# Per-chunk attention products as 64x64x64 tiles on quarters of the array

## The chip, the cores and the metric

The program runs on one core of a Trainium2 chip. The metric is the time of one execution on the device in microseconds, as the median of several runs. The profile is of one further execution of the same program; its span runs from its first to its last instruction. TensorE multiplies matrices out of SBUF into PSUM (8 banks of 2 KB in each of 128 partitions), VectorE, ScalarE and GpSimd work element by element, and SyncE's queue (SP) issues most of the transfers.

## What is computed

Attention within chunks of 64 positions, then two feed-forward stages:

```
scores = q_c k_c^T / 8                     # per batch, head, chunk: 64 x 64, head_dim 64
attn   = softmax(scores);  out = attn v_c  # 8 batches, 8 heads, 576 positions = 9 chunks
h      = x @ w_in                          # 4608 tokens, 512 -> 1024
ln     = layernorm(h * softmax(h)) * g_ln
y      = ln @ w_out                        # 1024 -> 512
result = (silu(y @ w_gate) * (y @ w_val)) @ w_out2   # 512 -> 1536 -> 512
```

## The kernel before

The 4608 tokens are 36 tiles of 128 tokens. A tile holds two chunks of 64 positions, and for each chunk all 8 heads. The first phase (to about 600 us) takes the tiles through attention, the first feed-forward stage and, in groups of three tiles, the product with w_out; it also converts weights and writes split copies of them to memory. The second phase is the gated stage and the output product.

The order of the first phase is written out by hand (`tc.manual_schedule()`, line 485), one call of `first_slot(t)` for the first four tiles and of `slot(t)` for the rest (lines 569 to 646). Each engine works its own list in the order in which the calls stand there; what one engine needs of another is waited for through semaphores that the framework sets, and matmuls into a PSUM bank also wait for readers of the same tile's data in that bank. A slot of the steady part has on TensorE, in this order: the scores of tile t+2 (line 258), the hidden product of tile t (line 327, 24 matmuls of 512 columns), the transposes of the layernorm of tile t-1 (line 397), probabilities times values of tile t+1 (line 300), 32 matmuls of the product with w_out (line 145), and the transposes of the probabilities of tile t+2 (line 290). In `first_slot` values stand directly behind scores, ahead of the softmax.

Both products on chunks run in fp32. With head_dim 64 and chunks of 64 a product of one head and one chunk is 64 x 64 x 64. The kernel handles the two chunks of a head in one call: the stationary operand has 128 rows (the two chunks' 64 rows each, one chunk below the other) and 64 columns, and the moving operand is block diagonal, 128 rows by 2 x 64 columns, with zeros where row and column belong to different chunks. These operands are `kbd` for the keys and `pbd` for the transposed probabilities (lines 237 and 238, two buffers each), zeroed once at the start (lines 411 to 413) and then filled in their diagonal blocks: `kbd` by two transfers per tile (line 245), `pbd` by two ScalarE copies of 64 partitions each (line 293). Even heads write the lower 64 PSUM partitions, odd heads the upper (`tile_position`). An fp32 matmul call of this form has two weight-load and two matmul records in the trace. Scores (`s`) and outputs (`o`) take the two one-bank buffers of the pool `ps_a` in turn.

`softmax` takes the row maximum and subtracts it on VectorE (lines 267 and 269) and exponentiates on ScalarE (272); `softmax_b` sums, and scales on GpSimd (282); `p_transpose` transposes on TensorE. `x_split` reads `o` twice, a copy on ScalarE (309) and a subtraction on VectorE (311), and makes the two-part input of the hidden product. `ln_max`, `ln_exp`, `ln_b` and `ln_c` (lines 339 to 381) follow the hidden product on VectorE, ScalarE and GpSimd. The PSUM pool `ps_y` has two buffers, which the products with w_out (emptied on ScalarE, line 151) and the transposed probabilities take in turn.

Of the kernel before, what the change touches and what calls it, by code (L numbers as in the profile page):

```python
# [8 lines left out]
F32 = mybir.dt.float32  # L9
# [4 lines left out]
AF = mybir.ActivationFunctionType  # L14
ALU = mybir.AluOpType
AX = mybir.AxisListType

P = 128
CH = 64
# [6 lines left out]
def attn_moe_moe2_kernel(  # L26
# [13 lines left out]
    nc = tc.nc  # L40
    NT = qT.shape[0]
    NG = NT // GT
    H = 8
    NP = H // 2
# [175 lines left out]
    with ExitStack() as ph1:  # L220
        wpool = ph1.enter_context(tc.tile_pool(name="wpool", bufs=1))
        wA = wblock(wpool, "A", 2 * KD)
        att = ph1.enter_context(tc.tile_pool(name="att", bufs=2))
        fix = ph1.enter_context(tc.tile_pool(name="fix", bufs=1))
        sm = ph1.enter_context(tc.tile_pool(name="sm", bufs=4))
        xp = ph1.enter_context(tc.tile_pool(name="xp", bufs=2))
        hp_ = ph1.enter_context(tc.tile_pool(name="hp", bufs=2))
        stage = ph1.enter_context(tc.tile_pool(name="stage", bufs=2))
        ps_a = ph1.enter_context(tc.tile_pool(name="ps_a", bufs=2, space=bass.MemoryType.PSUM))
        ps_h = ph1.enter_context(tc.tile_pool(name="ps_h", bufs=1, space=bass.MemoryType.PSUM))  # L230
        ps_t = ph1.enter_context(tc.tile_pool(name="ps_t", bufs=1, space=bass.MemoryType.PSUM))
        ps_y = ph1.enter_context(tc.tile_pool(name="ps_y", bufs=2, space=bass.MemoryType.PSUM))
# [1 line left out]
        qt, kt, vt, st, xt = {}, {}, {}, {}, {}  # L234


        kbd = [fix.tile([P, H, 2, CH], F32, name=f"kbd{i}") for i in range(2)]
        pbd = [fix.tile([P, H, 2, CH], F32, name=f"pbd{i}") for i in range(2)]

        def load_qk(t):  # L240
            qt[t] = att.tile([P, H, CH], F32, tag="qt", name="qt")
            nc.sync.dma_start(out=qt[t], in_=qT[t].rearrange("p (h i) -> p h i", h=H))
            for c in range(2):
                r = slice(c * CH, (c + 1) * CH)
                nc.sync.dma_start(
                    out=kbd[t % 2][r, :, c, :], in_=kT[t, r].rearrange("p (h j) -> p h j", h=H)
                )

        def load_v(t):
            vt[t] = att.tile([P, H, CH], F32, tag="vt", name="vt")  # L250
            nc.sync.dma_start(out=vt[t], in_=v[t].rearrange("p (h d) -> p h d", h=H))

        def scores(t):
            s = ps_a.tile([P, NP, 2, CH], F32, tag="a", name="s")
            q = qt.pop(t)
            for h in range(H):
                n, b = divmod(h, 2)
                nc.tensor.matmul(  # L258
                    s[b * CH:(b + 1) * CH, n], lhsT=q[:, h, :], rhs=kbd[t % 2][:, h],
                    start=True, stop=True, tile_position=(0, b * CH),  # L260
                )
            st[t] = s

        def softmax(t):
            s = st[t].rearrange("p n c j -> p (n c) j")
            mx = sm.tile([P, H], F32, tag="mx", name="mx")
            nc.vector.tensor_reduce(out=mx, in_=s, axis=AX.X, op=ALU.max)
            e = att.tile([P, H, CH], F32, tag="e", name="e")
            nc.vector.tensor_tensor(
                out=e, in0=s, in1=mx.unsqueeze(2).to_broadcast([P, H, CH]), op=ALU.subtract  # L270
            )
            nc.scalar.activation(out=e, in_=e, func=AF.Exp, scale=SCALE)
            st[t] = e
# [12 lines left out]
        def p_transpose(t):  # L286
            e = st.pop(t).rearrange("p (n c) j -> p n (c j)", c=2)
            pt = ps_y.tile([P, H, CH], F32, tag="y", name="pt")
            for n in range(NP):
                nc.tensor.transpose(pt[:, 2 * n:2 * n + 2].rearrange("p h i -> p (h i)"), e[:, n], ident)  # L290
            for c in range(2):
                r = slice(c * CH, (c + 1) * CH)
                nc.scalar.activation(out=pbd[t % 2][r, :, c], in_=pt[r], func=AF.Copy)

        def pv(t):
            vv = vt.pop(t)
            o = ps_a.tile([P, NP, 2, CH], F32, tag="a", name="o")
            for h in range(H):
                n, b = divmod(h, 2)
                nc.tensor.matmul(  # L300
                    o[b * CH:(b + 1) * CH, n], lhsT=vv[:, h, :], rhs=pbd[t % 2][:, h],
                    start=True, stop=True, tile_position=(0, b * CH),
                )
            st["o", t] = o

        def x_split(t):
            o = st.pop(("o", t)).rearrange("p n c i -> p n (c i)")
            x = xp.tile([P, 2, KD, P], F32R, tag="x", name="x")
            nc.scalar.activation(out=x[:, 0], in_=o, func=AF.Copy)
            xt[t] = x  # L310
            low = lambda: nc.vector.tensor_tensor(
                out=x[:, 1], in0=o, in1=x[:, 0].bitcast(F32), op=ALU.subtract
            )
            return low

# [92 lines left out]

        make_identity(nc, ident)
        nc.gpsimd.memset(mhalf, -0.5)  # L410
        for i in range(2):
            nc.gpsimd.memset(kbd[i], 0.0)
            nc.vector.memset(pbd[i], 0.0)
        rblk = [
            pool.tile([P, KD, DM], I64, tag=f"C{i}", name=f"rin{i}")
            for i, pool in enumerate((wpool, lastp))
# [5 lines left out]
        load_in(0)  # L422
        load_in(1)
        load_qk(0)
        load_in(2)
        load_qk(1)
        load_in(3)
        load_v(0)
# [12 lines left out]
        def y_upto(t):  # L441

            return max(0, min((NG - 1) * KD * NY, (t - GT) * KD * NY // GT)) if t >= W_OUT else 0
# [48 lines left out]
        word(1)  # L492
        add(1)
        scores(0)
        mag(2)
        clp(POOL, 2)
        high(0)
        rnd(2)
        high(1)
        softmax(0)  # L500
        rest(DVE, 0)
        word(2)
# [6 lines left out]
        high(2)  # L509
        rnd(4)  # L510
        p_transpose(0)
        word(3)
        add(3)
        rest(DVE, 2)
        scores(1)
        mag(5)
        clp(POOL, 5)
        word(4)
        add(4)
        high(3)  # L520
        pv(0)
        x_low = x_split(0)
        rest(DVE, 3)
        x_low()
# [17 lines left out]
        add(7)  # L542
        high(6)
        softmax(1)
        high(7)
        rest(DVE, 6)
        softmax_b(1)
        rest(DVE, 7)
        hidden(0, (1,))
        p_transpose(1)  # L550

        wB = wblock(lastp, "B", KF)
        raws = {0: w_raw(0)}
        load_qk(2)
        load_v(2)
        load_qk(3)
# [12 lines left out]
        def slot(t, todo2):  # L569
# [5 lines left out]
            if ahead:  # L575
                scores(t + 2)
                if t + 4 < NT:
                    load_qk(t + 4)
                softmax(t + 2)
# [12 lines left out]
            if t + 1 < NT:  # L592
                pv(t + 1)
                if t + 3 < NT:
                    load_v(t + 3)
                x_low = x_split(t + 1)
# [16 lines left out]
            if t + 2 < NT:  # L613
                raws[t + 2] = w_raw(t + 2)
                p_transpose(t + 2)
            return w_rest(todo, cs)

        def first_slot(t, todo2):

            todo = w_todo(t)  # L620
            cs = conv.pop(t)
            scores(t + 2)
            load_qk(t + 4)
            for k, steps in todo2:
                steps[1]()
            pv(t + 1)
            load_v(t + 3)
            softmax(t + 2)
            cs[:1] = [conv_c(c) for c in conv_b(cs[:1])]
            x_low = x_split(t + 1)  # L630
            softmax_b(t + 2)
            x_low()
            conv_start(t + 1)
            if t > 0:
                hidden(t)
            ln_max(t)
            ln_exp(t)
            cs[1:] = [conv_c(c) for c in conv_b(cs[1:])]
            ln_low = ln_T(t - 1) if t >= 1 else None
            ln_b(t)  # L640
            p_transpose(t + 2)
            if ln_low:
                ln_low()
            ln_c(t)
            raws[t + 2] = w_raw(t + 2)
            return w_rest(todo, cs)
# [17 lines left out]
        n = y_upto(NT - 1)  # L664
# [236 lines left out]
```

## Time and profile before

| | |
|---|---|
| three runs | 1431.06, 1431.95, 1433.1 us |
| median | 1431.95 us |
| the profiled execution's own time | 1430.28 us |
| its span | 1428.5 us |
| mean granted TensorE clock | 0.989 of full |
| TensorE busy, matmuls | 1376.6 us (96%) |
| TensorE busy, weight loads | 1251.2 us (88%) |
| VectorE, ScalarE, GpSimd busy | 846.2, 585.9, 469.8 us |
| scores and values matmuls (lines 258, 300) | 44.2 and 42.2 us busy |

Busy time is the union of an engine's records. A matmul's record goes on after the next one has begun, so a stage of TensorE is read from its first start to the first start of the next stage. A granted clock of 1.00 is 2.4 GHz and of 0.50 is 1.2 GHz; values between are a mean over a stretch with both. In a group's or a timeline's row, a bracket or the columns behind the bar name the idle time ahead of it and what ended it ("issue" is nothing that the profile shows).

### The profile page before, as it was taken

How to read it: one execution, taken by the hardware profiler on the slowest of the kernel's cores; microseconds unless marked ns; L12 is line 12 of the kernel's file. 1: busy time of each engine (PE TensorE's matmuls, PEld its weight loads, DVE VectorE, ACT ScalarE, POOL GpSimd, SP SyncE). 2: the span in 40 equal slices, each digit the busy share in tenths (PEclk: the TensorE clock that was granted, in tenths of full speed). 3: DMA queues.
4: the chain of work that ended last, by engine and by line, in shares of the span. 5: the costliest groups of instructions: out<-in, count | busy, mean ns of one | idle time of the engine just before them, and what ended most of it. 6: DMA issues, size and time to landing. Idle time of an engine off the chain costs nothing.

```text
span 1428.5 us, 21447 instructions
## 1 busy us (share of the span) xinstructions
PE 1376.6 (96%) x7920; PEld 1251.2 (88%) x7920; DVE 846.2 (59%) x1534; ACT 585.9 (41%) x1172; POOL 469.8 (33%) x591
## 2 busy tenths in 40 slices
PE   4789999999999999899999999999999999999998
PEld 3668888888888889899989998999999899989997
DVE  7876677777676666554474456445544644474442
ACT  5754555655555555432332333323323323233231
POOL 5643444444453443421231223213212412141120
PEclk9799999999999999999999999999999999999999
DMA  7433655546475553876645473455455454735531
GB/s 257 126 94 99 186 163 167 179 128 202 132 208 158 151 163 113 329 299 240 224 146 196 167 246 137 171 202 203 147 203 205 153 192 165 247 125 179 203 106 45
DMA packets 123128, 252.02 MB, mean 176 GB/s; under 512 B 45712, under 2 KB 79504, under 8 KB 113808
## 3 DMA queue, kind: packets, MB, share of 16 engines
q1 hardware_dynamic: 116112, 241.21, 50.6%
q10 hardware_dynamic: 6912, 9.44, 1.9%
q8 instruction: 63, 1.03, 0.3%
q14 instruction: 41, 0.34, 0.1%
HBM read 203.43 MB, written 47.19 MB: 175 GB/s over the span
## 4 chain that ended last, share of the span: by engine, by line
PE 76%; DVE 2%; ACT 1%; POOL 1%; issue 1%; ACTq 0%; DVEq 0%; POOLq 0%
PE o L799 14%; PE pa L733 11%; PE pd L733 10%; PE pc L733 10%; PE h L327 8%; PE y L145 7%; PE tail L799 7%; PE pb L733 5%; PE s L258 1%; PE o L300 1%; PE tr L397 1%; PE pt L290 1%; DVE so L357 0%; DVE nm L339 0%; ACT eh L346 0%
## 5 line engine op out<-in xcount | busy, mean ns | idle before, releaser
L327 PE MATMUL h<-wA,x 128*128 128x512 f32 x864 | 214.3, 404 | 6.3 <-DVE wA L480 2.5
L145 PE MATMUL y<-lnT,wB 128*128 128x384 f32 x1152 | 211.8, 340 | 5.2 <-DVE lnT L405 3.8
L145 PEld LDWEIGHTS y<-lnT,wB 128*128 128x128 f32 x1152 | 200.5, 190 | 11.6 <-issue 5.3
L790 POOL TENSOR_TENSOR uflow<-sa,uflow 128x384 fp32r<-128x384 f32 x72 | 73.4, 1019 | 414.4 <-ACT uflow L761 393.2
L327 PEld LDWEIGHTS h<-wA,x 128*128 128x128 f32 x864 | 163.3, 193 | 48.2 <-issue 5.8
L733 PE MATMUL pa<-yk,wsa 128*128 128x384 f32 x864 | 175.0, 337 | 0.8 <-DVE osb L816 0.8
L733 PE MATMUL pd<-yk,wsb 128*128 128x384 f32 x864 | 172.9, 334 | 0.0
L790 DVE TENSOR_TENSOR uflow<-sb,uflow 128x128 fp32r<-128x128 f32 x72 | 28.1, 391 | 228.9 <-ACT uflow L788 228.9
L733 PEld LDWEIGHTS pa<-yk,wsa 128*128 128x128 f32 x864 | 153.2, 188 | 7.6 <-DVE osb L816 2.9
L733 PEld LDWEIGHTS pd<-yk,wsb 128*128 128x128 f32 x864 | 151.8, 188 | 0.0
L769 POOL TENSOR_TENSOR u<-u,p 128x384 f32<-128x384 f32 x72 | 72.9, 1013 | 193.5 <-DVE u L768 189.6
L758 ACT ACTIVATE p<-pa 128x384 f32<-128x384 f32 x72 | 35.4, 492 | 232.7 <-PE pa L733 231.0
L799 PE MATMUL o<-wo,uflow 128*128 128x512 f32 x504 | 122.8, 392 | 0.0
L799 PEld LDWEIGHTS o<-wo,uflow 128*128 128x128 f32 x504 | 94.0, 188 | 18.1
L346 ACT ACTIVATE eh<-h,nm 128x1024 f32<-128x1024 f32 x36 | 40.1, 1115 | 155.0 <-DVE nm L339 155.0
L771 ACT ACTIVATE sa<-pa 128x384 f32<-128x384 f32 x72 | 35.5, 492 | 150.0 <-PE pa L733 150.0
L799 PE MATMUL o<-uflow 128*128 128x512 f32 x360 | 87.4, 391 | 0.0
L733 PE MATMUL pc<-yk,wsa 128*128 128x384 f32 x432 | 86.4, 334 | 0.0
L733 PE MATMUL pb<-yk,wsa 128*128 128x384 f32 x432 | 86.4, 334 | 0.0
L733 PE MATMUL pc<-yk,wsb 128*128 128x384 f32 x432 | 86.4, 334 | 0.0
L772 DVE TENSOR_TENSOR sa<-pa,sa 128x384 f32<-128x384 f32 x72 | 40.1, 557 | 71.6 <-ACT sa L771 71.6
L799 PEld LDWEIGHTS o<-uflow 128*128 128x128 f32 x360 | 67.2, 188 | 13.2
(107 smaller groups left out, 2361.6 us busy)
## 6 DMA issues: line engine op xcount, KB each, us to landing
wsa<-ws SPq DMA_DIRECT2D x72, 1024.0 KB, 5.0
wsb<-ws SPq DMA_DIRECT2D x72, 768.0 KB, 5.9
ws<-shi SPq DMA_DIRECT2D x12, 896.0 KB, 4.5
raw<-in_moe_w_out SPq DMA_DIRECT2D x20, 512.0 KB, 5.1
qt<-in_q SPq DMA_DIRECT2D x36, 256.0 KB, 4.7
kbd<-in_k SPq DMA_DIRECT2D x72, 128.0 KB, 4.9
vt<-in_v SPq DMA_DIRECT2D x36, 256.0 KB, 2.8
y<-ysb ACTq DMA_DIRECT2D x48, 192.0 KB, 2.1
```

What stands on the lines that cost most here:

```text
L145: nc.tensor.matmul(ys[u], lhsT=wB[:, f, a, d * P:(d + 1) * P], rhs=lnT[m][:, b, f, :], start=(n == 0), stop=(n == NY - 1),)
L258: nc.tensor.matmul(s[b * CH:(b + 1) * CH, n], lhsT=q[:, h, :], rhs=kbd[t % 2][:, h], start=True, stop=True, tile_position=(0, b * CH),)
L290: nc.tensor.transpose(pt[:, 2 * n:2 * n + 2].rearrange("p h i -> p (h i)"), e[:, n], ident)
L327: nc.tensor.matmul(h[:, n * DM:(n + 1) * DM], lhsT=x[:, a, k, :], rhs=wA[:, n * KD + k, b, :], start=(i == 0), stop=(i == 3 * KD - 1),)
L346: nc.scalar.activation(out=e, in_=h, func=AF.Exp, bias=nm, accum_out=se)
L733: nc.tensor.matmul(ps, lhsT=w[:, a, kk * P:(kk + 1) * P], rhs=yk[:, i, b, kk], start=(first and n == 0), stop=(n == 5), skip_group_check=True,
L758: nc.scalar.activation(out=p1, in_=psA, func=AF.Copy)
L769: nc.gpsimd.tensor_tensor(out=u3, in0=u3, in1=p5, op=ALU.add)
L771: nc.scalar.activation(out=sa, in_=psA, func=AF.Sigmoid)
L772: nc.vector.tensor_tensor(out=sa, in0=psA, in1=sa, op=ALU.mult)
L790: sub = lambda eng, o, x, h: eng.tensor_tensor(out=o, in0=x, in1=h.bitcast(F32), op=ALU.subtract)
L799: nc.tensor.matmul(o, lhsT=u[:, a, i * P:(i + 1) * P], rhs=wout(f)[:, b], start=(j0 and j == 0), stop=(j1 and j == 2),)
```

## The change

Each of the two products becomes 16 calls of 64 x 64 x 64 per tile, one for each head and chunk. A call uses 64 rows of the array (the chunk's) and 64 columns (by the head's parity). Keys and transposed probabilities are kept without zeros in [128, 8, 64] tiles, loaded by one transfer and written by one copy; the block-diagonal tiles, their memsets and their pool go. In PSUM a chunk has a bank of its own; scores take one half of each of the two banks and outputs the other half, in one tile that lives through the phase. The softmax and `x_split` read the new order of chunks and heads through other views.

```diff
-        ps_a = ph1.enter_context(tc.tile_pool(name="ps_a", bufs=2, space=bass.MemoryType.PSUM))
+        ps_a = ph1.enter_context(tc.tile_pool(name="ps_a", bufs=1, space=bass.MemoryType.PSUM))
...
-        kbd = [fix.tile([P, H, 2, CH], F32, name=f"kbd{i}") for i in range(2)]
-        pbd = [fix.tile([P, H, 2, CH], F32, name=f"pbd{i}") for i in range(2)]
+        so_ps = ps_a.tile([P, 2, 2, NP, CH], F32, name="so_ps")
+        s_ps, o_ps = so_ps[:, :, 0], so_ps[:, :, 1]
+        quads = [(n, c, b) for n in range(NP) for c in range(2) for b in range(2)]
+
+        def quad(out, lhsT, rhs, n, c, b):
+
+            r, h = slice(c * CH, (c + 1) * CH), 2 * n + b
+            nc.tensor.matmul(
+                out[b * CH:(b + 1) * CH, c, n], lhsT=lhsT[r, h], rhs=rhs[r, h],
+                start=True, stop=True, tile_position=(c * CH, b * CH),
+            )
...
-            for c in range(2):
-                r = slice(c * CH, (c + 1) * CH)
-                nc.sync.dma_start(
-                    out=kbd[t % 2][r, :, c, :], in_=kT[t, r].rearrange("p (h j) -> p h j", h=H)
-                )
+            kt[t] = att.tile([P, H, CH], F32, tag="kt", name="kt")
+            nc.sync.dma_start(out=kt[t], in_=kT[t].rearrange("p (h j) -> p h j", h=H))
...
-            s = ps_a.tile([P, NP, 2, CH], F32, tag="a", name="s")
-            q = qt.pop(t)
-            for h in range(H):
-                n, b = divmod(h, 2)
-                nc.tensor.matmul(
-                    s[b * CH:(b + 1) * CH, n], lhsT=q[:, h, :], rhs=kbd[t % 2][:, h],
-                    start=True, stop=True, tile_position=(0, b * CH),
-                )
-            st[t] = s
+            q, k = qt.pop(t), kt.pop(t)
+            for i in quads:
+                quad(s_ps, q, k, *i)
...
-            s = st[t].rearrange("p n c j -> p (n c) j")
-            mx = sm.tile([P, H], F32, tag="mx", name="mx")
-            nc.vector.tensor_reduce(out=mx, in_=s, axis=AX.X, op=ALU.max)
+            mx = sm.tile([P, 2, NP], F32, tag="mx", name="mx")
+            nc.vector.tensor_reduce(out=mx, in_=s_ps, axis=AX.X, op=ALU.max)
             e = att.tile([P, H, CH], F32, tag="e", name="e")
             nc.vector.tensor_tensor(
-                out=e, in0=s, in1=mx.unsqueeze(2).to_broadcast([P, H, CH]), op=ALU.subtract
+                out=e.rearrange("p (n c) j -> p c n j", c=2), in0=s_ps,
+                in1=mx.unsqueeze(3).to_broadcast([P, 2, NP, CH]), op=ALU.subtract,
             )
...
-            for c in range(2):
-                r = slice(c * CH, (c + 1) * CH)
-                nc.scalar.activation(out=pbd[t % 2][r, :, c], in_=pt[r], func=AF.Copy)
+            p = att.tile([P, H, CH], F32, tag="p", name="p")
+            nc.scalar.activation(out=p, in_=pt, func=AF.Copy)
+            st["p", t] = p
...
-            vv = vt.pop(t)
-            o = ps_a.tile([P, NP, 2, CH], F32, tag="a", name="o")
-            for h in range(H):
-                n, b = divmod(h, 2)
-                nc.tensor.matmul(
-                    o[b * CH:(b + 1) * CH, n], lhsT=vv[:, h, :], rhs=pbd[t % 2][:, h],
-                    start=True, stop=True, tile_position=(0, b * CH),
-                )
-            st["o", t] = o
+            vv, p = vt.pop(t), st.pop(("p", t))
+            for i in quads:
+                quad(o_ps, vv, p, *i)
...
-            o = st.pop(("o", t)).rearrange("p n c i -> p n (c i)")
+            o = o_ps.rearrange("p c n i -> p n c i")
             x = xp.tile([P, 2, KD, P], F32R, tag="x", name="x")
-            nc.scalar.activation(out=x[:, 0], in_=o, func=AF.Copy)
+            hi, lo = (x[:, i].rearrange("p n (c i) -> p n c i", c=2) for i in range(2))
+            nc.scalar.activation(out=hi, in_=o, func=AF.Copy)
...
-        for i in range(2):
-            nc.gpsimd.memset(kbd[i], 0.0)
-            nc.vector.memset(pbd[i], 0.0)
```

## Rows read from the trace of the kernel before

**Rows 1.** Stretches (us): length, busy time (records) per engine, PE clock, DMA.

```profile
30.00:60.00 30.00, 20.36 (x130) 15.83 (x130) 23.25 (x41) 19.42 (x35) 17.08 (x21) 0.78 0.36 106
102.09:545.26 443.17, 432.00 (x2897) 378.77 (x2897) 306.25 (x547) 240.88 (x424) 190.38 (x296) 1.00 0.53 158
600.00:1428.00 828.00, 823.91 (x4323) 768.55 (x4321) 426.64 (x809) 256.84 (x594) 194.71 (x184) 1.00 0.52 185
```

**Rows 2.** Timeline, TensorE, one steady slot: start us, us, what, records.

```profile
301.18 1.09 PE L258 MATMUL s<-kbd,qt 128*64 128x128 f32 x16
302.21 5.75 PE L327 MATMUL h<-wA,x 128*128 128x512 f32 x24
...
308.76 1.09 PE L300 MATMUL o<-pbd,vt 128*64 128x128 f32 x16
309.79 5.82 PE L145 MATMUL y<-lnT,wB 128*128 128x384 f32 x32
```

**Rows 3.** Groups, TensorE, 100 to 560 us: records | busy us, mean ns.

```profile
L300 PE MATMUL o<-pbd,vt 128*64 128x128 f32 x480 | 32.8, 279 | 0.0
L258 PE MATMUL s<-kbd,qt 128*64 128x128 f32 x464 | 32.2, 282 | 0.0
```

**Rows 4.** Short stretches, records on tile s: length, PE busy, loads, VectorE.

```profile
301.17:301.20 0.03, 0.02 (x2) 0.02 (x2) 0.00 (x0) 1.00 0.00 0
...
301.33:301.36 0.03, 0.03 (x4) 0.03 (x4) 0.00 (x0) 1.00 0.00 0
...
301.44:301.47 0.03, 0.03 (x6) 0.03 (x4) 0.00 (x0) 1.00 0.00 0
```

**Rows 5.** Groups, weight loads (PEld), 100 to 560 us.

```profile
L327 PEld LDWEIGHTS h<-wA,x 128*128 128x128 f32 x727 | 134.9, 189 | 32.8 <-issue 5.1
...
L258 PEld LDWEIGHTS s<-kbd,qt 128*64 128x64 f32 x464 | 25.1, 138 | 4.8 <-issue 4.8
```

**Rows 6.** Waits, TensorE, 100 to 560 us: total us, times, longest.

```profile
PE pt L290 <- ACT ysb L151: 6.0, 3, 2.6
PE pt L290 <- POOL rs L380: 3.5, 4, 1.5
PE pt L290 <- POOL so L381: 1.5, 1, 1.5
```

**Rows 7.** Chain that ended last, 361 to 376 us: start, us.

```profile
361.81 5.70 PE h L327 x24
...
367.53 1.24 DVE nm L339
...
375.45 0.38 ACT ysb L151
```

**Rows 8.** A stretch after a long wait, and the chain behind it.

```profile
469.80:471.40 1.60, 1.60 (x18) 1.24 (x17) 0.00 (x0) 1.18 (x2) 0.88 (x2) 0.65 1.03 337
...
471.42 6.76 PE h L327 x24
```

**Rows 9.** Timeline of the same slot: readers of scores and outputs, next scores.

```profile
303.05 0.69 DVE L269 TENSOR_TENSOR e<-s,mx 128x512 f32<-128x512 f32 x1
...
313.57 0.68 DVE L311 TENSOR_TENSOR x<-o,x 128x512 fp32r<-128x512 f32 x1
...
315.98 1.09 PE L258 MATMUL s<-kbd,qt 128*64 128x128 f32 x16
```

**Rows 10.** Timeline of the start: idle time before and its releaser in brackets.

```profile
0.89 1.84 POOL L412 MEMSET kbd<- 128x1024 f32 x2
...
7.83 1.97 PE L258 MATMUL s<-kbd,qt 128*64 128x128 f32 x16 [7.83 <-DMA kbd<-in_k]
...
9.85 0.69 DVE L267 TENSOR_REDUCE mx<-s 128x8 f32<-128x512 f32 x1 [0.88 <-PE s L258]
```

**Rows 11.** Timeline of the opening, 72 to 75 us, ScalarE and TensorE.

```profile
72.16 1.19 ACT L293 ACTIVATE pbd<-pt 64x512 f32<-64x512 f32 x2
...
73.40 1.13 PE L300 MATMUL o<-pbd,vt 128*64 128x128 f32 x16 [2.26 <-ACT pbd L293]
```

More of the change, by code (lines that the diff above doesn't have):

```diff
@@ L223, in attn_moe_moe2_kernel @@
         att = ph1.enter_context(tc.tile_pool(name="att", bufs=2))
-        fix = ph1.enter_context(tc.tile_pool(name="fix", bufs=1))
         sm = ph1.enter_context(tc.tile_pool(name="sm", bufs=4))
@@ L290, in p_transpose @@
                 nc.tensor.transpose(pt[:, 2 * n:2 * n + 2].rearrange("p h i -> p (h i)"), e[:, n], ident)
-            for c in range(2):
-                r = slice(c * CH, (c + 1) * CH)
-                nc.scalar.activation(out=pbd[t % 2][r, :, c], in_=pt[r], func=AF.Copy)
+            p = att.tile([P, H, CH], F32, tag="p", name="p")
+            nc.scalar.activation(out=p, in_=pt, func=AF.Copy)
+            st["p", t] = p
         def pv(t):
-            vv = vt.pop(t)
-            o = ps_a.tile([P, NP, 2, CH], F32, tag="a", name="o")
-            for h in range(H):
-                n, b = divmod(h, 2)
-                nc.tensor.matmul(
-                    o[b * CH:(b + 1) * CH, n], lhsT=vv[:, h, :], rhs=pbd[t % 2][:, h],
-                    start=True, stop=True, tile_position=(0, b * CH),
-                )
-            st["o", t] = o
+            vv, p = vt.pop(t), st.pop(("p", t))
+            for i in quads:
+                quad(o_ps, vv, p, *i)
         def x_split(t):
-            o = st.pop(("o", t)).rearrange("p n c i -> p n (c i)")
+            o = o_ps.rearrange("p c n i -> p n c i")
             x = xp.tile([P, 2, KD, P], F32R, tag="x", name="x")
-            nc.scalar.activation(out=x[:, 0], in_=o, func=AF.Copy)
+            hi, lo = (x[:, i].rearrange("p n (c i) -> p n c i", c=2) for i in range(2))
+            nc.scalar.activation(out=hi, in_=o, func=AF.Copy)
             xt[t] = x
             low = lambda: nc.vector.tensor_tensor(
-                out=x[:, 1], in0=o, in1=x[:, 0].bitcast(F32), op=ALU.subtract
+                out=lo, in0=o, in1=hi.bitcast(F32), op=ALU.subtract
             )
```

## The prediction

> **What bounds the kernel now.** I read the table of stretches first [rows 1]. From 102 to 545 us, the 30 steady slots of the first phase, TensorE is busy 432.0 of 443.2 us at full clock, while VectorE has 306, ScalarE 241 and GpSimd 190: TensorE's own work sets the pace. From 600 us on it is busy 824 of 828 us, and nothing there is edited. Only in the opening is another engine tighter: between 30 and 60 us VectorE is busy 23.3 of 30 us, TensorE 20.4, at a granted clock of 0.78.
>
> Next I read one slot on TensorE in order of time [rows 2]. The scores begin at 301.18 and the hidden matmuls at 302.21: the score stage holds TensorE for 1.03 us. The values stage runs from 308.76 to 309.79: 1.03 us again. The stretch has 29 score stages and 30 values stages (464 and 480 records of 16) [rows 3], about 60 us in all. That is what the change can shorten.
>
> Then I looked inside one score stage with very short stretches [rows 4]; the counts are records that touch the stretch. Two begin at 301.18, two more by 301.36, two more by 301.47. So records begin in twos, one two per 0.11 us: 8 steps, 0.88 us. The other 0.15 us of the stage lies at its two ends, where the first weights are loaded and the last results leave. Each of the 8 calls has two records of 128 columns. I read a two as the left and the right half of the array at work together, each passing 128 columns in a step.
>
> **The change, part by part.**
>
> *The two products.* A stage goes from 8 calls with 128 rows, 64 weight columns and 128 moving columns to 16 calls of 64 by 64 by 64, four places in place of two. Records go from 16 to 32. If four run together, there are again 8 steps, each with 64 columns, so half as long: 0.055 us. The weight load must fit under it. A 128-column load has a mean of 189 ns and a 64-column load 138 ns [rows 5], so 64 columns are worth 51 ns: just under the step. I take 0.06 us, since there is almost nothing to spare: 8 x 0.06 = 0.48 in place of 0.88, a gain of 0.40 us per stage. The ends: 0.44 us with 0.055, and 0 with the step of today.
> All of a score stage's gain reaches the end, as the hidden matmuls follow at once: 29 x 0.40 = 11.6 us. A values stage's gain is lost where the probability transposes later wait for something else than TensorE. They do so eight times in the stretch [rows 6]. The chain of waits shows why [rows 7]: it leaves TensorE at the end of the hidden matmuls (367.5), passes through the maximum on VectorE and a line of work on ScalarE, and comes back when ScalarE has emptied a PSUM tile at 375.8. The values stage lies beside that chain. So 30 - 8 = 22 stages count: 22 x 0.40 = 8.8 us.
> Those eight waits grow by 0.40 us each. After one of them, at 469.8, the clock was granted at 0.65 and a score stage took 1.6 us, the hidden matmuls behind it 6.76 us in place of 5.7 [rows 8]: 1.6 us lost in all. I set 1 us against the gain for more of this; ends 0 and 3.
>
> *Scores and outputs share two PSUM banks.* A matmul into a bank waits for the readers of the bank's other half. Scores would now wait for the subtraction that ends x_split two slots before: it ends at 314.25 and the scores begin at 315.98, 1.7 us of room, of which the shorter values stage takes 0.4. The values product waits for the softmax's subtraction, which ends at 303.74, while the product begins at 308.76 [rows 2, 9]. Behind those waits stands all of TensorE, but the room covers them: 0. In the first four slots values come directly behind scores, so that the row maximum now waits for both; the two shorter stages together last about as long as one did: 0.
>
> *Zeros and copies.* The memsets of kbd hold GpSimd from 0.89 to 2.73 us, ahead of the key loads. The first scores begin at 7.83, when the keys land, and VectorE then waits 0.88 us for them [rows 10]. An earlier key load and a shorter stage at half clock can take that wait away and no more than a little beyond: I take 1 us; ends 0 and 3. VectorE's memsets of pbd lie before its first job. The two half copies into pbd (1.19 us together) become one copy over 128 partitions with as many columns as one of them, 0.6 us less on ScalarE. Where values wait for them, as at 73.4 (2.26 us) [rows 11], the opening's tighter VectorE is next: I take 0.5 us in all; ends 0 and 2.
> The key load is one transfer in place of two, so that the SP queue has one issue less per slot; it lands well ahead of its use after the start, and its cover is the slots it is loaded ahead: 0. VectorE and ScalarE read and write as many elements as before in another order; their room in the stretch [rows 1] hides what that might cost.
>
> *Sum.* 11.6 + 8.8 + 1 + 0.5 - 1 = 20.9 us. The profiled execution took 1430.28 us (span 1428.5), which gives 1409.4. It lies 1.67 us under the median of the three runs, 1431.95. Against the median: **1411 us**.
>
> **The rivals.**
>
> *A, four places are no faster than two.* A two could be the two records of one call, one call at a time; then 16 calls make 16 steps of 0.055 us, 0.88 us as now. Left are the start and the copies: 1430.5. For it: 8 calls in 8 steps fit as well. Against it: one record needs the step for its own 128 columns, and two of them in one place would share it.
> The Trainium skill, page "TensorE: Matmul & The Clock Gate", Part 3, says that matmuls start and end strictly in program order and only weight loads are pulled ahead. By that, a call's second half would hold back the next call, and the new stage would have 17 steps, 0.935 us: 59 x 0.055 = 3.2 us more than in A, about 1434. The trace speaks against it: 8 calls would then take nine steps with a single record at each end, and the stage begins with two [rows 4].
>
> *B, records have a pace of their own.* On average one begins every 0.055 us now. If that is the rate at which TensorE takes them, and not what the columns need, 32 records take 1.76 us, 0.88 more per stage: 59 x 0.88 = 52 us, less 1.5 for the start and the copies: **1482 us**. It decides from 0.0275 us per record on, where 32 of them take the 0.88 us of today. For it: no stage of this trace runs faster than this average. Against it: two begin within one stretch of 0.03 us [rows 4], so the pace between them is far quicker.
>
> *C, the chain outside TensorE takes over.* If maximum, exponential and the work after them bound every slot, only the score stages gain: 11.6 + 1.5 = 13.1 us, 1419. Against it: all of TensorE's idle time in the stretch is 11 us [rows 1, 6].
>
> **How the numbers follow.** My forecast has 0.58: column tiles of today begin together, and nothing in the rows sets a quarter apart from a half. A has 0.16, B 0.16 (it can stop anywhere between 1435 and 1482), C 0.10. The forecast's own range: at best 59 x 0.44 + 3 + 2 = 31, so about 1401; at worst 1420, with a step a quarter longer than 0.06, nothing from the start and 3 us lost to low clock (51 x 0.28 - 3 = 11). The range runs from 1402 to 1433: it takes in C and nearly all of A, and leaves out B and the edge of the forecast. Within 0.2% is 2.9 us, about what can be told from no change. Faster: forecast and C, 0.68. Same: A, 0.16. Slower: B, 0.16.
>
> **What would show it.** Right: in a slot, from the scores' first record to the first hidden matmul about 0.64 us in place of 1.03, starts in fours, a slot of about 14.0 us, still eight or more waits of the transposes for ScalarE's copies, each some 0.4 us longer. Wrong: starts in twos every 0.055 us (A), single starts at an even pace with the stage over 1.03 us (B), VectorE named before the scores (the shared banks), or low clock after the longer waits.

## The result, and the profile after

| | before | after |
|---|---|---|
| time, median of 6 runs each, taken together | 1432.73 us (1431.06 to 1433.32) | **1420.04 us** (1416.62 to 1424.49) |
| ratio of the runs | | **0.9915**, 95% interval 0.9892 to 0.9937 |
| profiled execution: time, span, mean granted clock | 1430.28 us, 1428.5 us, 0.989 | 1421.21 us, 1419.4 us, 0.982 |

The kernel became 12 to 13 us faster (9 to 15 by the interval), not the 21 that were forecast. The time lies inside the range given, on the side forecast.

The timeline of TensorE in the changed kernel, the slot that answers to [rows 2] (start us, us, what, records):

```profile
300.58 0.69 PE L243 MATMUL so_ps<-kt,qt 64*64 64x64 f32 x32
301.20 5.75 PE L321 MATMUL h<-wA,x 128*128 128x512 f32 x24
...
307.75 0.69 PE L243 MATMUL so_ps<-p,vt 64*64 64x64 f32 x32
308.38 5.84 PE L145 MATMUL y<-lnT,wB 128*128 128x384 f32 x32
...
314.59 0.69 PE L243 MATMUL so_ps<-kt,qt 64*64 64x64 f32 x32
```

Each product stage, from its first record to the first of the matmuls behind it, went from 1.03 to 0.62 or 0.63 us, and this slot from scores to scores lasts 14.01 us in place of 14.80. The gain per stage is 0.40 to 0.41 us, and 0.40 was forecast.

Inside one score stage, the short stretches that answer to [rows 4] (the counts are the records that touch the stretch):

```profile
300.57:300.60 0.03, 0.02 (x3) 0.02 (x4) 0.00 (x0) 0.00 (x0) 1.00 0.04 0
300.73:300.76 0.03, 0.03 (x11) 0.03 (x10) 0.00 (x0) 0.00 (x0) 1.00 0.00 0
```

The start times of the 32 records behind these counts are 300.580, .587, .593 and .600, then 300.687, .693, .700 and .707, then 300.745, .752, .758 and .765, and so on in fours: four starts 7 ns apart, eight fours, and after the first a new four every 0.058 us. A call has two records. The trace does not name the quarter of a record; I read a four as four calls on the four quarters, one record of each, and the reordered calls below bear that out. The Trainium skill, page "TensorE: Matmul & The Clock Gate", Part 3, says that matmuls start in program order; by that the second record of a call would hold back the first of the next call, as rival A worked out. Here the trace does not agree, as far as the two records of a call stand next to each other in the program: the stage has eight steps and not seventeen.

So the mechanism is the one forecast. Whether the columns or the weight loads set the 0.058 us is not shown. What was given back shows first in the waits of TensorE, 100 to 560 us (total us, times, longest), against 6.0, 3.5 and 1.5 in [rows 6]:

```profile
PE pt L289 <- ACT ysb L151: 9.2, 4, 3.0
PE pt L289 <- POOL rs L374: 6.5, 4, 1.9
PE pt L289 <- POOL rs L367: 0.4, 1, 0.4
```

The releaser in such a row is inferred. In the kernel the transposes use nothing of `rs`, a short chain on GpSimd; they take the PSUM tile that ScalarE empties as `ysb`, and at 148 us that copy ended at 148.27 and the transposes began at 148.38. So I count all nine as waits for ScalarE's copies.

It shows, second, in the table of stretches (length, TensorE busy with its records, granted clock, DMA). The first line is the stretch of [rows 1], where the clock was 1.00; the others are 2 us each, after the opening's last waits and after four of the nine waits for the transposes:

```profile
102.09:545.26 443.17, 427.03 (x3923) 0.98 0.50 164
...
100.90:102.90 2.00, 2.00 (x7) 0.50 0.00 0
148.70:150.70 2.00, 2.00 (x37) 0.50 1.03 336
196.50:198.50 2.00, 2.00 (x5) 0.50 1.05 346
285.30:287.30 2.00, 2.00 (x35) 0.50 0.68 260
462.80:464.80 2.00, 2.00 (x5) 0.50 1.04 348
```

A clock of 0.50 is 1.2 GHz. Before, only one wait in the steady part, the one at 469.8, was followed by it [rows 8]; now there are four. What one costs shows where the timeline of the changed kernel passes the second of them (idle time before and its releaser in brackets):

```profile
195.12 0.63 PE L289 MATMUL pt<-ident,e 128*128 128x128 f32 x4 [3.00 <-ACT ysb L151]
195.69 0.69 PE L243 MATMUL so_ps<-kt,qt 64*64 64x64 f32 x32
196.31 7.35 PE L321 MATMUL h<-wA,x 128*128 128x512 f32 x24
...
211.27 0.69 PE L243 MATMUL so_ps<-kt,qt 64*64 64x64 f32 x32
```

The hidden matmuls took 7.35 in place of 5.75 us, and the slot 15.58 in place of 14.01. The last slot of the opening shows the same loss, here in the changed kernel and then in the kernel before:

```profile
84.99 8.31 PE L321 MATMUL h<-wA,x 128*128 128x512 f32 x24 [2.29 <-DVE so L351]
...
99.84 0.61 PE L145 MATMUL y<-lnT,wB 128*128 128x384 f32 x2 [1.69 <-ACT wB L124]
100.63 3.91 PE L145 MATMUL y<-lnT,wB 128*128 128x384 f32 x12 [0.18 <-DVE wB L125]
...
104.91 0.69 PE L243 MATMUL so_ps<-kt,qt 64*64 64x64 f32 x32
```

```profile
86.18 5.73 PE L327 MATMUL h<-wA,x 128*128 128x512 f32 x24 [1.99 <-DVE so L357]
...
99.23 2.49 PE L145 MATMUL y<-lnT,wB 128*128 128x384 f32 x12 [0.18 <-DVE wB L125]
```

The first of these groups took 8.31 in place of 5.73 us and the last 3.91 in place of 2.49.

**The account** of the two profiled executions, from the starts of the score stages (before 83.09, 102.09 and 530.99 us; after 82.00, 104.91 and 521.12):

| where | gain, us |
|---|---|
| up to the seventh score stage (83.09 against 82.00) | +1.1 |
| the opening's last slot, 19.00 against 22.91 | -3.9 |
| 28 steady slots, products: 28 x (14.795 - 14.01) | +22.0 |
| the same slots, waits for the transposes: 16.1 against 11.0 | -5.1 |
| the same slots, low clock after the waits: the rest of 428.90 - 416.21 = 12.7 | -4.2 |
| after the last score stage (a wait of 1.6 us for ScalarE before a group of the second phase at 595 among it) | -0.8 |
| sum, as the two executions (1430.28 - 1421.21) | +9.1 |

The low clock of the steady slots is what the other two terms leave. Read slot by slot, the changed kernel lost 1.5 to 1.6 us at each of four waits, 6.1 in all, and the kernel before 1.6 at one: 4.5 us. The opening's loss is that of one execution; the first experiment shows how far it moves.

### The profile page after: what moved, and what is told of

It reads as the page before. It is cut to its first block, busy times and chain, and to the rows that moved or that the text cites. A ratio compares the mean times of both kernels' runs of the same rounds, so it can differ in the third digit from the quotient of the medians.

```text
span 1419.4 us, 23604 instructions
## 1 busy us (share of the span) xinstructions
PE 1353.7 (95%) x9072; PEld 1233.8 (87%) x9072; DVE 845.6 (60%) x1532; ACT 563.6 (40%) x1136; POOL 468.6 (33%) x589
## 4 chain that ended last, share of the span: by engine, by line
PE 58%; DMA 2%; DVE 0%; ACT 0%; issue 0%; SPq 0%; ACTq 0%; DVEq 0%
PE o L790 14%; PE pa L724 11%; PE pd L724 10%; PE pc L724 10%; PE tail L790 7%; PE pb L724 5%; DMA wsa<-ws 1%; DMA y<-ysb 1%; DMA ws<-blk 0%; DMA rawy<-y 0%; DVE osb L807 0%; DVE m L209 0%; ACT wohi L204 0%; ACT osb L805 0%; ACT p L749 0%
## 5 line engine op out<-in xcount | busy, mean ns | idle before, releaser
L321 PE MATMUL h<-wA,x 128*128 128x512 f32 x864 | 220.1, 412 | 7.0 <-DVE wA L471 2.7
L321 PEld LDWEIGHTS h<-wA,x 128*128 128x128 f32 x864 | 167.8, 198 | 46.6 <-DVE wA L471 3.8
L790 PEld LDWEIGHTS o<-uflow 128*128 128x128 f32 x360 | 67.2, 188 | 13.2
```

The source lines that it names most:

```text
L321: nc.tensor.matmul(h[:, n * DM:(n + 1) * DM], lhsT=x[:, a, k, :], rhs=wA[:, n * KD + k, b, :], start=(i == 0), stop=(i == 3 * KD - 1),)
L790: nc.tensor.matmul(o, lhsT=u[:, a, i * P:(i + 1) * P], rhs=wout(f)[:, b], start=(j0 and j == 0), stop=(j1 and j == 2),)
```

## The experiments

The theory: TensorE's own work became shorter as forecast. Where a slot's end waits for the chain through maximum, exponential and ScalarE's copies, the shorter work only lengthens TensorE's wait, and the longer waits now bring the low clock more often. The rivals: the loss is only the longer waiting; or the four quarters hold each other up; or other engines bound the slot.

**Spare work ahead of the waits.** In eight slots that end in a long wait, two more passes of score products go ahead of the transposes. Their sums are overwritten by the real scores.

```diff
+FILL = (7, 10, 13, 16, 22, 25, 28, 31)
...
+                if t in FILL and t + 3 < NT:
+                    for i in 2 * quads:
+                        quad(s_ps, qt[t + 3], kt[t + 3], *i)
                 p_transpose(t + 2)
```

> Theory (the clock): in the changed kernel the transposes' waits are longer than before, four of them last 2 us or more, and behind each of those the granted clock falls to half, so that the score stage and the hidden matmuls behind it lose some 1.5 to 2 us. Here two spare passes over the score quarters (about 1.1 us of work with no use) stand in eight of the nine slots ahead of the waiting transposes; the waits' ends do not move. Then no half clock shows between 100 and 560 us, and the time falls by about 6 us against the changed kernel, to about 1414. Rival (the waits alone): what was given back lies in the waits themselves; the spare work changes nothing within 2 us, about 1420. Rival (TensorE's work sets the pace everywhere): eight times 1.1 us more work, about 1429.

Measured: **1410.63 us** (1408.58 to 1413.13), ratio to the kernel before 0.9856 (0.9841 to 0.9872): 9.4 us faster than the change (8 us, when each is set against the kernel before that ran beside it), with more work in it. The timeline at the wait that corresponds to the one shown above, and the table of stretches (length, TensorE, clock, DMA):

```profile
188.24 1.16 PE L244 MATMUL so_ps<-kt,qt 64*64 64x64 f32 x64
191.35 0.63 PE L290 MATMUL pt<-ident,e 128*128 128x128 f32 x4 [1.95 <-ACT ysb L152]
191.91 0.69 PE L244 MATMUL so_ps<-kt,qt 64*64 64x64 f32 x32
192.53 5.78 PE L322 MATMUL h<-wA,x 128*128 128x512 f32 x24
```

```profile
102.09:545.26 443.17, 435.32 (x4465) 1.00 0.51 167
```

The wait is 1.95 in place of 3.00 us and ends where it did, 16.7 us behind the slot's first scores (16.6 in the changed kernel); the clock stays at 1.00, and the hidden matmuls take 5.78 us. In the profiled executions 5.6 of the 10.6 us lie between the hidden matmuls of the sixth and of the last slot (442.2 against 436.6 us), where the spare work is. The other 5.0 lie outside: 2.4 before, where the two programs are the same, and 2.6 behind. The opening's last slot took 20.13 us here and 22.91 in the changed kernel, with the same program up to its end. So the opening's loss differs from one execution or build to the next, and the clock after the waits was worth some 5 us.

**The same spare work elsewhere,** as a control: in eight slots that end without a long wait.

```diff
-FILL = (7, 10, 13, 16, 22, 25, 28, 31)
+FILL = (6, 9, 12, 15, 21, 24, 27, 30)
```

> The changed kernel with the same spare score products as in the filled kernel (two passes of all the calls, eight times), but in eight slots that end without a long wait of TensorE, so that the eight long waits stay as they are in the changed kernel. If the filled kernel's gain came from TensorE being kept at work where it otherwise waited (the clock's theory), nothing is won here and the spare work is paid for: 8 times about 1.0 us on 1420, so about 1428 (1424 to 1433), with the half clock still after the waits at 148, 196, 285 and 462 us and a mean granted clock near 0.982. If the spare work helps for another reason (any shift of TensorE against the other engines, or more work anywhere), the time is 1410 to 1419 here too, and the half clock is gone from 100 to 560 us.

Measured: 1423.41 us (1419.35 to 1426.5), ratio 0.994 (0.9918 to 0.9962), mean clock 0.983. The table of stretches, behind two of its waits; behind those at 288 and 469 us the clock is 0.50 too:

```profile
196.50:198.50 2.00, 2.00 (x36) 0.50 1.04 340
...
421.80:423.80 2.00, 2.00 (x35) 0.50 1.03 339
```

Nothing is won, and the low clock stays after four waits, though not after the same four (421 in place of 148). That the time lies just under the range of the theory has a plain reason in the slots: a filled one lasts 15.25 us in place of 14.01, but two slots with a small wait behind it fell from 15.56 to 14.82, as the spare work ate that wait. So it is the place of the spare work that made the first kernel faster, and not the work. In four of its slots the low clock came after waits of 3.0, 1.7, 1.9 and 3.0 us; after another of 1.9, at 150 us, it did not.

**The same calls in another order.** The calls of one half of the rows first, then those of the other.

```diff
-        quads = [(n, c, b) for n in range(NP) for c in range(2) for b in range(2)]
+        quads = [(n, c, b) for c in range(2) for n in range(NP) for b in range(2)]
```

> The calls of a stage are issued all of the first chunk, then all of the second, in place of four quarters in turn. Theory (a matmul begins as soon as its own quarter is free, and the queue is looked through far enough): starts still come in fours, a stage lasts 0.62 us, the time is that of the changed kernel, about 1420. Rival (only calls that stand close together in the queue run together): starts come in twos, a stage lasts about 8 x 2 x 0.058 + 0.15 = 1.08 us as in the kernel before; the time goes back to about 1432 or slightly above.

Measured: 1431.43 us (1427.91 to 1434.75), ratio 1.0002 (0.9993 to 1.0011): the whole gain is gone. The timeline of one score stage, and the stretches inside it, at its beginning and in its middle:

```profile
304.56 0.98 PE L243 MATMUL so_ps<-kt,qt 64*64 64x64 f32 x32
305.47 5.74 PE L321 MATMUL h<-wA,x 128*128 128x512 f32 x24
```

```profile
304.56:304.60 0.04, 0.04 (x2) 0.04 (x2) 0.00 (x0) 0.00 (x0) 1.00 0.00 0
304.60:304.64 0.04, 0.04 (x2) 0.04 (x4) 0.00 (x0) 0.00 (x0) 1.00 2.09 410
304.90:304.93 0.03, 0.03 (x10) 0.03 (x10) 0.00 (x0) 0.00 (x0) 1.00 0.00 0
```

A stage takes 0.91 us, between the two values expected. It begins in twos, and only in its middle, from 304.85 to 305.03, where the two halves of the list meet, do records start in fours. I read this as follows: TensorE does look past a call whose quarter is taken, since the second half's twos begin beside those of the first half that are still to come, but not over the whole list. The stage's gain is largest with the four quarters side by side in program order, as the change has them.

That the whole 12 us went is not the order of the calls alone. A stage still gains 0.12 us on the kernel before, and a steady slot takes 14.54 us in place of 14.80, which makes 7 us over 28 slots. In the profiled execution the low clock and the opening took this back: the two slots behind the waits at 197 and 470 us took 17.39 and 17.46 us, where the kernel before had one such slot of 16.38, and the opening's last slot 23.16 in place of 19.00.

**The transposes later.** In the steady slots the transposes of the probabilities leave the end of the slot, where they waited, and stand behind the next hidden matmuls; done to both kernels.

```diff
             if t > 0:
                 hidden(t)
+            if t > W_OUT and t + 1 < NT:
+                p_transpose(t + 1)
             ln_max(t)
...
-                p_transpose(t + 2)
```

> The changed kernel with the probability transposes of a tile issued behind the next slot's hidden matmuls (from the fifth slot on) and not ahead of its scores, so that TensorE has 6 us of other work while ScalarE empties the PSUM tile they wait for. Theory (waits and clock): the nine waits (17.6 us in the changed kernel) and the low clock behind them go; slots of about 14.0 us throughout; about 1420 - 17 - 6 = 1397. Rival (another wait takes their place, the values product for ScalarE's copy of the transposed probabilities, or the products with w_out for their PSUM tile): slots over 14.3 us, and 1405 to 1420.

> The kernel before with the same move of the transposes. Theory (waits and clock): its nine waits (12.4 us) and the one low clock behind them go: slots of 14.8 us throughout, about 1432 - 12 - 2 = 1418; the distance to the changed kernel with the same move is then the products' own gain, 60 stages x 0.41 = 24 us less what the opening gives back. Rival (the products' gain is smaller than the stages show): the distance stays near the 12 us between the two kernels without the move.

Measured, on the changed kernel: **1393.08 us** (1391.58 to 1395.0), ratio 0.9733 (0.972 to 0.9747). It beats both kernels. It is 4 us under the time expected, which fits the opening: its last slot took 18.48 us here, at full clock, in place of 22.91. (The 17.6 us of waits in the expectation are taken from start to start of the stages and so hold the ends of the last y matmuls; idle time alone is 16.1.) No wait for the transposes is left, and 28 slots in a row take 14.04 us each:

```profile
303.38 0.60 PE L289 MATMUL pt<-ident,e 128*128 128x128 f32 x4
303.81 1.04 PE L391 MATMUL tr<-ident,so 128*128 128x128 f32 x8
304.78 0.69 PE L243 MATMUL so_ps<-p,vt 64*64 64x64 f32 x32
305.41 5.84 PE L145 MATMUL y<-lnT,wB 128*128 128x384 f32 x32
311.18 0.69 PE L243 MATMUL so_ps<-kt,qt 64*64 64x64 f32 x32
```

On the kernel before: 1432.67 us (1430.46 to 1436.37), ratio 1.0011 (1.0002 to 1.0019): no gain where 14 us were expected. Its waits from 100 to 560 us, and the timelines of TensorE and of ScalarE there:

```profile
PE o L300 <- ACT pbd L293: 12.5, 30, 0.4
```

```profile
308.58 0.60 PE L290 MATMUL pt<-ident,e 128*128 128x128 f32 x4
309.01 1.04 PE L397 MATMUL tr<-ident,so 128*128 128x128 f32 x8
310.46 1.09 PE L300 MATMUL o<-pbd,vt 128*64 128x128 f32 x16 [0.41 <-ACT pbd L293]
```

```profile
309.21 1.20 ACT L293 ACTIVATE pbd<-pt 64x512 f32<-64x512 f32 x2 [3.97 <-PE pt L290]
```

Thirty waits of 0.4 us took the place of the eight longer ones: behind the transposes there lies now only 1 us of other matmuls, and the two half copies into the block diagonal, one after the other, take 1.20. The changed kernel has one copy of 0.6 us, which fits.

**The half copies side by side,** to test that: in the kernel before with late transposes, the second one goes to VectorE.

```diff
-            for c in range(2):
-                r = slice(c * CH, (c + 1) * CH)
-                nc.scalar.activation(out=pbd[t % 2][r, :, c], in_=pt[r], func=AF.Copy)
+            nc.scalar.activation(out=pbd[t % 2][:CH, :, 0], in_=pt[:CH], func=AF.Copy)
+            nc.vector.tensor_copy(pbd[t % 2][CH:, :, 1], pt[CH:])
```

> The kernel before with the transposes of the probabilities moved behind the hidden layer, and the second of the two half copies into the block diagonal given to VectorE, so that the two copies (1.19 us each) run beside each other in place of one after the other. If the two serial copies were what took the place of the removed waits, the wait of the values products for them goes from 0.4 us a slot to nearly none, the slots go from 15.29 to about 14.8, and the time is about 1418 (1412 to 1424). If VectorE's own queue holds the copy back as long, the slots stay at 15.0 to 15.4 and the time is 1425 to 1436, with the wait of the values products now put down to DVE.

Measured: 1440.44 us (1439.05 to 1440.94), ratio 1.0062 (1.0045 to 1.0079), slower than either expectation. The copies did not run side by side, as the timelines of ScalarE and of VectorE show:

```profile
312.71 0.59 ACT L291 ACTIVATE pbd<-pt 64x512 f32<-64x512 f32 x1 [3.97 <-PE pt L290]
```

```profile
313.34 0.69 DVE L292 COPY pbd<-pt 64x512 f32<-64x512 f32 x1 [0.62 <-ACT pbd L291]
```

VectorE waited for ScalarE's copy, and its own takes 0.69 us in place of 0.59 (that both write one tile is the likely reason, not tried); the wait of the values products grew to 0.54 us. The edit did not do what it was meant to do, so its time says nothing against the cause; it shows that 0.12 us more of copying (1.32 from the first copy's start to the second's end, in place of 1.20) is 0.14 us more of slot (15.43 in place of 15.29).

**The transposes between the halves of the hidden layer,** the better test: half a hidden layer covers the copies; done to both kernels.

```diff
             if t > 0:
-                hidden(t)
+                hidden(t, (0,))
             if t > W_OUT and t + 1 < NT:
                 p_transpose(t + 1)
+            if t > 0:
+                hidden(t, (1,))
             ln_max(t)
...
-                p_transpose(t + 2)
```

> The kernel before with the transposes of the probabilities between the two halves of the hidden layer, so that half a hidden layer (2.9 us) lies behind them to cover the two serial half copies (1.2 us). If the wait of 0.4 us a slot for these copies is what kept the kernel before from gaining by late transposes, the values products wait no more, the steady slots go from 15.29 to about 14.85 us, and the time is about 1418 (1414 to 1423). If a slot of this kernel is bound by something else outside TensorE, slots stay at 15.1 or more and the time at 1427 to 1436.

> The changed kernel with the same order. There the copy of the probabilities was covered already when the transposes stood behind the hidden layer, so the steady slots stay at 14.04 us and the time at 1393 (1391 to 1395). The distance to the kernel before in the same order is then what the products on quarters are worth by themselves with no wait and no half clock between: two stages of 0.41 us in each of about 32 slots, 26 us (22 to 29). If the products' own gain were smaller than the stages show (because work beside them takes it back), the distance is under 18 us.

Measured: 1419.42 us (1417.85 to 1422.08) on the kernel before, ratio 0.9917 (0.9894 to 0.994), and 1395.28 us (1394.81 to 1397.7) on the changed one, 0.9746 (0.9726 to 0.9765). The stretches of 300 to 400 us (length, TensorE, clock, DMA), of the kernel before and then of the changed one:

```profile
300.00:400.00 100.00, 100.00 (x684) 1.00 0.59 176
```

```profile
300.00:400.00 100.00, 100.00 (x960) 1.00 0.57 188
```

TensorE never rests in either, at full clock. The steady slots take 14.83 and 14.10 us. The distance of the two kernels, 24.1 us, is what the products on quarters are worth without the waits: nearly twice the 12.7 of the change as it was made, and near the 59 x 0.41 = 24.2 us of the stages. That it agrees so closely is in part chance. In the two profiled executions (22.9 us apart) the steady slots differ by 0.73 and not by 0.82 us, 20.3 us over 28 slots, in part because the hidden halves take 0.05 us more beside the quarters; the opening took 0.7 us back, and 3.3 came from the last score stage on, 1.2 of them products, the rest a low clock and a wait of 0.95 us in the kernel before that have little to do with the products. And the kernel before gains 13.2 us from the order by itself. The changed kernel came out 2.3 us over the 1393 expected, mostly because its slots take 0.06 us more in this order than with the transposes behind the hidden matmuls.

**The opening.** The changed kernel with late transposes, and spare products ahead of the waits up to 100 us, written to a tile that nobody reads.

```diff
+        def fill(t, n):
+            junk = ps_y.tile([P, NP, CH], F32, tag="y", name="junk")
+            for m, c, b in n * [i for i in quads if i[1] == 0]:
...
+            if t == W_OUT:
+                fill(t + 3, 3)
...
+            if t > 0:
+                fill(t + 3, (0, 3, 1, 3)[t])
```

> The changed kernel with the transposes moved behind the hidden layer (1393.1 us), and spare products on two quarters in the opening ahead of the waits up to 100 us. If the half clock at 32, 56 and 73 us costs time there, these stretches go and the time falls by 1 to 4 us, to 1389 to 1392. If the opening waits for VectorE and the transfers whatever TensorE's clock is, the granted clock rises in 30 to 100 us and the time stays at 1393 to 1395.

Measured: 1392.91 us (1391.69 to 1392.99), ratio 0.9727 (0.9713 to 0.9742): no change against 1393.08. The stretches of the opening, without the spare products and then with them:

```profile
30.00:60.00 30.00, 18.02 (x242) 0.71 0.33 107
60.00:100.00 40.00, 32.37 (x262) 0.92 0.30 99
```

```profile
30.00:60.00 30.00, 21.01 (x293) 0.77 0.34 110
60.00:100.00 40.00, 34.30 (x369) 0.91 0.29 97
```

The clock rose only from 0.71 to 0.77 between 30 and 60 us and not at all after, so this is no real test; it shows only that this much clock is worth nothing there. Whether the opening's 3.9 us in the account can be kept from being lost was not settled; nor was why the low clock falls there in some executions.

## Why the prediction was right, and what it missed

- **The products** were right: the stage of 0.62 us (0.64 forecast), the step of 0.058 us (0.06), starts in fours, slots of 14.01 us (14.0). Rivals A and B fell with the starts: two more records side by side cost 0.014 us and no step. The reordered calls show that A was nearer than it looked: another order of the same sixteen calls gives a stage of 0.91 us, nearer to the 1.03 of A (0.88 of steps and 0.15 of ends) than to 0.62.
- **Eight waits that swallow the values stage's gain** were right in kind and too small in size. The eight waits and a ninth, at 328 us (0.4 us, before 0.1), came to 5.1 us more than [rows 6], not to 8 x 0.40 = 3.2. Most grew by 0.3 to 0.5 us; two, at 240 and 506 us, by 1.1. At the first of these VectorE's queue is late. Its timeline in the changed kernel:

```profile
231.51 0.83 DVE L278 TENSOR_SCALAR su<-su 128x8 f32<-128x8 f32 x1
...
232.50 1.17 DVE L333 TENSOR_REDUCE nm<-h 128x1 f32<-128x1024 f32 x1
```

  The maximum over h starts at 232.50 with no idle time before it, while TensorE had left the hidden matmuls for the next group at 231.49: in this slot VectorE, not the hidden layer, set when the chain to the next wait began. This was read from the trace and not tried by itself.
- **The low clock** is the term that failed: "I set 1 us against the gain for more of this; ends 0 and 3". It measured 4.2 us in the steady slots, and the 3.9 us of the opening's last slot belong to it too (8.31 against 5.73 us and 3.91 against 2.49 us in two groups, 4.0 in all): some 8 us in that execution, where the worst end of the term was 3. Up to 3 of the 8, in the opening, come and go from one execution to the next. One slot behind one wait was taken as the pattern; but with every wait longer more of them cost, three in the steady part that had cost nothing before. "Low clock after the longer waits" was among the prediction's own signs of being wrong, and it came. That the clock takes this time, beside the longer waits themselves, is shown by the spare work ahead of the waits (5.6 us between the sixth and the last hidden matmuls, with the ends of the waits where they were) and its control (1423.4 us). Why it follows one wait and not another of the same length stays open.
- **The time** came out at the worst end that the forecast gave itself, 1420 us, but not by that end's terms: it had a step a quarter longer and 3 us of low clock, and the runs showed the whole gain of the step and more low clock. The range reached to 1433 to take in two rivals, so that the time lies within it says little for the low clock's term.
- **The start** was right: 1.1 us earlier by the seventh score stage, of 1.5 forecast for start and copies. **The shared banks** cost nothing that the trace shows.
- Of the forecast 20.9 us and the 9.1 of the profiled executions, the difference of 11.8 is: low clock with the opening 7.1 (4.2 + 3.9 - 1.0), waits 1.9 (5.1 - 3.2), the end of the first phase 0.8, the start and the copies 0.4, and 1.6 of the products (23.6 - 22.0), of which 0.8 lies in the opening's slot, whose two stages gained too.
- **Rival C** got the time almost to the microsecond (1419) and is not what happened. TensorE's idle time bounds no slot without a wait, and both stages gain wherever none follows.

## What to carry to other kernels

A shorter job on the engine that bounds a kernel pays in full only where nothing waits behind it: look for the waits that it lengthens first, and move those (here a reorder that is worth 13 us in the kernel before is worth 25 in the changed one). On TensorE a wait that grows from 2.6 to 3.0 us, or from 1.5 to 1.9, can cost more than its length (here 1.5 to 1.6 us each at four of nine waits), by the low clock after it; price that for every wait that grows, not for the one where it shows already. And an order of the calls is part of such a change: the same sixteen products took 0.62 or 0.91 us a stage by how they followed each other, and the kernel gained 12 us or nothing, the rest being lost to the clock.

## What the runs showed that was not expected

- Spare matmuls made a kernel 8 to 9 us faster, by standing ahead of the waits, and in eight other slots made it no faster.
- A low clock does not follow the length of the wait alone: after waits of 1.9 and 2.1 us it came at 148 and 285 us, after one of 1.9 us at 416 it did not; in the kernel before it came after the wait of 2.6 us at 469 and not after that of 2.6 at 195. What it takes is much the same each time: behind the wait of 3.0 us at 195 the hidden matmuls lost 1.6 us, behind the one at 148 they lost 0.76, but there the transposes and scores ahead of them had lost 0.32 and 0.44.
- The six runs of the changed kernel spread over 7.9 us and stand in the order of their mean granted clocks: 0.985 at 1416.6 and 1416.7 us, 0.982 at 1418.9 and 1421.2, 0.981 at 1423.9, 0.979 at 1424.5. The four runs of the version with late transposes spread over 3.4.
- Four 64 x 64 products start 7 ns apart on the four quarters, and a new four begins every 0.058 us, just over half of the 0.109 us for 128 columns.
